# Attention and a gated mixer in one kernel: row sums from a ones column in V, scalings on two engines, V's rows ordered by SBUF loads

## The chip, the cores and the metric

The kernel runs on one core of a Trainium2 chip. A core has five engines that run their own instruction lists side by side: TensorE (PE; its weight loads are listed as PEld), VectorE (DVE), ScalarE (ACT), GpSimd (POOL) and SyncE (SP, which here only issues transfers). SBUF is the core's memory of 128 partitions; PSUM, eight banks of 2 KB per partition, takes the results of TensorE. The metric is the device time of one execution in microseconds (us), lower is better.

## The reference

There are 2048 tokens of width 448 in bf16. First comes an attention block: every token looks at eight tokens, itself and those 2, 4, ..., 14 positions before it. Then comes a gated mixer whose spatial product mixes all 2048 tokens.

```
def _A_ref(x, wqkv, wo):                 # H = 16 heads of Dh = 28
    W, dil = (8, 2)
    qkv = (x @ wqkv).reshape(B, S, 3, H, Dh) ...
    idx = pos[:, None] - (arange(W) * dil)[None, :];  mask = idx >= 0
    logits = einsum('bhsd,bhswd->bhsw', q, k[idx]) * Dh ** -0.5
    attn = softmax(where(mask, logits, -1e9))
    return einsum('bhsw,bhswd->bhsd', attn, v[idx]) ... @ wo

def _B_ref(x, w_in, w_sp, b_sp, w_out):  # Fh = 896
    z = gelu(x @ w_in);  z1 = z[..., :Fh];  z2 = layernorm(z[..., Fh:])
    g = einsum('ts,bsf->btf', w_sp, z2) + b_sp[None, :, None]
    return (z1 * g) @ w_out

h  = x + _A_ref(layernorm(x), wqkv, wo)
h2 = h + _B_ref(layernorm(h), w_in, w_sp, b_sp, w_out)
```

## The kernel before, in words

**Layout.** The 2048 tokens are 16 blocks of 128. A unit u (0 to 7) is the pair of blocks u and u + 8. xh (L421) holds the normalized input transposed: features on partitions, the first 1024 tokens on partitions 0 to 63 and the second 1024 on 64 to 127, so that two products with a contraction of 64 stand side by side for the two halves. The work goes from the last unit to the first.

**First layer norm (ln_unit, L634).** For each block statistics on VectorE (bn, L640, L645), 1/sqrt(var + eps) on POOL (L629, L630) or on ScalarE as Ln and Exp (L656, L657), and the scaling to tring on VectorE (nrm, L664). Then the transpose: units 7, 6 and 5 on PE with a copy from PSUM, units 4 to 0 by a DMA transpose issued on SP (L671). The second layer norm, of h, uses the same function with all eight units transposed by DMA. Blocks wait in a ring of four tring buffers.

**Q, K and V.** Q and K are computed in three chunks of tokens (L776) from padded weights wpd, which VectorE and ScalarE copy out of staged loads. V is computed in nine tiles of 114 tokens with a halo of 14 (L826). Since the attention looks at every second token, a tile's V must stand with even tokens on partitions 0 to 63 and odd ones on 64 to 127. To get this, the kernel before copies the tile's columns of xh, reordered, into xv (L816; two buffers, on VectorE or ScalarE), and uses xv as the stationary operand. V itself is copied from PSUM into one of three buffers (L838) whose heads are 32 wide: 28 values and four zeros.

**A tile of attention (i = 8 down to 0).** Two groups of 32 logit products (mml, L857), two Exp (L871) into E, two multiplies by the band mask on VectorE (L879), eight products of E with a matrix of ones (mmr, L892), which give each row's sum on all 32 rows of its head, a Ln and an Exp(-x) on ScalarE for the reciprocal in L (L901, L926), 64 value products E times V (mmo, L915), and the multiply by the reciprocal out of PSUM into oT on VectorE (ot, L934).

**Behind it.** For each unit the output projection (mmy, L978), the residual add into x_tm (h, L987), the second layer norm, two z2 groups (L999) with a GELU on ScalarE (L1009), the statistics of z2 (L1015, L1021) and its scaling (nrm3, L1029, VectorE). The z1 groups (L1042) have their own GELU (L1052). Then the spatial product g (L1076) in 28 groups of 16, the bias add and the gate on VectorE (L1086, L1093), and the output product (L1103), add (L1111) and store (L1115). The transposed loads of w_sp (L959) are chained: each waits for the one before it.

**What sets the order.** Every piece of work is a task. SEQ (L48) gives, for each of the five engines, the order of its tasks, written out by number. replay (L299) walks these lists with estimated costs, hands out PSUM banks and ring buffers, and records the instructions; each engine runs its list in order and waits on semaphores where it must. All loads, transposes and stores but two stand in SP's one list. When PE waits for long at the start, replay puts in matmuls on a constant tile to keep PE's clock (L618).

## Time and profile before

| | |
|---|---|
| median of three runs | 242.56 us (242.48 to 242.93) |
| the profiled execution | 242.51 us |
| its span | 240.8 us |
| granted clock of TensorE | 1.00 |
| PE busy | 233.3 us, 97% |
| VectorE busy | 136.7 us, 57% |
| ScalarE busy | 91.1 us, 38% |
| POOL busy | 24.9 us, 10% |
| moved by DMA | 22.52 MB |

The page gives busy time by engine, groups of equal instructions ("L879 DVE TENSOR_TENSOR out<-in" with its count, the busy time, the mean in ns of one, the idle time before and what ended it), and the chain that ended last. In a table of windows each row is a stretch of the span in us with the busy time and count of instructions of every engine in it, PE's granted clock, the busy share of the DMA engines and GB/s. A line of the timeline gives start, duration, engine, line, operation, tile and count. Lines of transfers give KB each and the us from issue to landing. Matmuls overlap, so that the sum of the durations of single ones is more than the time of a group; the chain has the time of a group.

### The profile page before, as it was taken

Reading aid. Unit: us, or ns where it says so; the run is one execution under the profiler, and the core shown is the slowest. Engines: PE = TensorE matmul, PEld = TensorE weight load, DVE = VectorE, ACT = ScalarE, POOL = GpSimd, SP = SyncE. Lnnn points to the kernel's source line nnn. Section 1 sums busy time; section 2 is a strip of 40 time slices with the busy share of each in tenths; the row PEclk is TensorE's granted clock in tenths of the full one; section 3 lists DMA queues with packets and bytes.
Section 4 is the critical chain, followed back from the end, with each engine's and each line's share of the span. In section 5 each row is a group of like instructions: output and inputs, shape, how many; then the busy total and the mean of one; then the engine's idle time right before and its main releaser. Section 6 shows DMA issues by size and latency. Waiting matters only on the chain.

```text
span 240.8 us, 6345 instructions
## 1 busy us (share of the span) xinstructions
PE 233.3 (97%) x2838; PEld 122.0 (51%) x2838; DVE 136.7 (57%) x288; ACT 91.1 (38%) x108; POOL 24.9 (10%) x66
## 2 busy tenths in 40 slices
PE   8889999999999999999999999999999999999994
PEld 2567754545556655555444444444444444444552
DVE  4989667699999995194951012235115522053743
ACT  2899877669998458965430000000000000000000
POOL 7114100001111133025120000000000000000000
PEclk9999999999999999999999999999999999999999
DMA  6959995293294959776844333000000100000034
GB/s 179 298 180 151 189 185 110 67 220 71 46 124 86 203 164 156 159 134 131 158 94 94 74 80 73 0 0 3 0 0 0 57 3 0 0 0 3 0 114 135
DMA packets 56558, 22.52 MB, mean 94 GB/s; under 512 B 46930, under 2 KB 56402, under 8 KB 56530
## 3 DMA queue, kind: packets, MB, share of 16 engines
q1 hardware_dynamic: 56242, 21.88, 43.6%
q8 instruction: 22, 0.36, 0.6%
q10 hardware_dynamic: 288, 0.23, 0.3%
q14 instruction: 6, 0.05, 0.1%
HBM read 8.90 MB, written 1.84 MB: 45 GB/s over the span
## 4 chain that ended last, share of the span: by engine, by line
PE 83%; DVE 9%; DMA 3%; SPq 2%; issue 1%; ACT 0%; DVEq 0%
PE psum L1076 40%; PE psum L776 9%; PE psum L999 9%; PE psum L1042 9%; PE psum L1103 6%; PE psum L826 4%; PE psum L978 3%; DMA z2p<-in_A_wqkv_dram 2%; DVE x_tm L987 2%; DVE st L640 2%; DVE reg L934 1%; DMA out_dram<-tring 1%; DVE reg L879 1%; PE psum L857 1%; PE psum L915 1%
## 5 line engine op out<-in xcount | busy, mean ns | idle before, releaser
L1086 DVE TENSOR_TENSOR reg<-psum,reg 128x512 bf16<-128x512 f32 x28 | 18.7, 687 | 62.2 <-PE psum L1076 62.1
L1076 PE MATMUL psum<-wspT_lo,z2p 128*128 128x512 bf16 x224 | 49.3, 379 | 0.0
L1076 PE MATMUL psum<-reg,z2p 128*128 128x512 bf16 x224 | 49.3, 379 | 0.0
L1076 PEld LDWEIGHTS psum<-wspT_lo,z2p 128*128 128x128 bf16 x224 | 21.8, 98 | 26.5 <-DVE st L1015 0.4
L1076 PEld LDWEIGHTS psum<-reg,z2p 128*128 128x128 bf16 x224 | 21.9, 98 | 26.3
L776 PE MATMUL psum<-xh,reg 64*128 64x256 bf16 (+2 forms) x336 | 25.6, 306 | 1.2 <-DVE reg L626 0.6
L999 PE MATMUL psum<-w_in,xh 64*128 64x448 bf16 x224 | 22.5, 349 | 0.1
L1103 PE MATMUL psum<-reg 128*128 128x448 bf16 (+1 forms) x119 | 22.3, 341 | 0.0
L1042 PE MATMUL psum<-xh,w_in 64*128 64x512 bf16 x196 | 21.9, 376 | 0.0
L1015 DVE BATCH_NORM_STATS2 st<-z2p 128x6 f32<-128x448 bf16 x32 | 17.7, 609 | 7.1 <-ACT z2p L1009 7.1
L776 PEld LDWEIGHTS psum<-xh,reg 64*128 64x128 bf16 x336 | 16.2, 94 | 9.2 <-DVE reg L626 1.2
L640 DVE BATCH_NORM_STATS2 st<-x_tm 128x6 f32<-128x448 bf16 x32 | 18.9, 613 | 2.3 <-DMA x_tm<-in_A_x_dram 2.2
L624 ACT ACTIVATE reg<-psum 128x1024 bf16<-128x1024 f32 (+2 forms) x19 | 17.1, 917 | 4.8 <-PE psum L776 4.7
L1052 ACT ACTIVATE reg<-psum 128x1024 bf16<-128x1024 f32 x14 | 13.8, 1029 | 12.2 <-PE psum L1042 12.2
L1111 DVE TENSOR_TENSOR tring<-psum,x_tm 128x448 bf16<-128x448 f32 (+1 forms) x17 | 9.6, 592 | 15.1 <-PE psum L1103 13.3
L871 ACT ACTIVATE reg<-psum 128x928 bf16<-128x928 f32 x18 | 16.2, 943 | 4.0 <-PE psum L857 4.0
L999 PEld LDWEIGHTS psum<-w_in,xh 64*128 64x128 bf16 x224 | 12.4, 94 | 9.0 <-issue 0.6
L1103 PEld LDWEIGHTS psum<-reg 128*128 128x128 bf16 x119 | 11.6, 98 | 10.0
L1042 PEld LDWEIGHTS psum<-xh,w_in 64*128 64x128 bf16 x196 | 11.1, 94 | 9.9 <-ACT reg L1052 0.2
L630 POOL TENSOR_TENSOR rs<-rs,nhalf 128x2 f32<-128x2 f32 x20 | 14.9, 746 | 1.7
L1009 ACT ACTIVATE z2p<-psum 128x896 bf16<-128x896 f32 x16 | 13.8, 927 | 3.2 <-PE psum L999 3.1
L629 POOL TENSOR_SCALAR rs<-mv 128x2 f32<-128x2 f32 x20 | 5.1, 254 | 94.1 <-DVE mv L645 71.7
(59 smaller groups left out, 201.6 us busy)
## 6 DMA issues: line engine op xcount, KB each, us to landing
w_in<-in_B_w_in_dram SPq DMA_DIRECT2D x4, 672.0 KB, 5.8
out_dram<-tring SPq DMA_DIRECT2D x15, 112.0 KB, 1.8
x_tm<-in_A_x_dram SPq DMA_DIRECT2D x6, 224.0 KB, 5.6
z2p<-in_A_wqkv_dram SPq DMA_DIRECT2D x3, 336.0 KB, 5.6
reg<-in_B_w_out_dram SPq DMA_DIRECT2D x1, 784.0 KB, 4.5
reg<-in_A_wqkv_dram SPq DMA_DIRECT2D x2, 336.0 KB, 6.1
reg<-in_B_b_sp_dram SPq DMA_DIRECT2D x1, 512.0 KB, 5.5
w_in<-in_B_w_in_dram SPq DMA_DIRECT2D x4, 112.0 KB, 4.8
```

The costliest lines, as they stand in the source:

```text
L624: iss("act", lambda e: e.activation(dst, src, AF.Copy), reads=rd, writes=wr)
L630: iss("pool", lambda e: e.tensor_tensor(dst, dst, nh, ALU.pow), reads=rr + [r_nhalf], writes=rr)
L640: iss("dve", lambda e: e.bn_stats(st[:, b, :], x_tm[:, b, :]), reads=[r_x[b]], writes=[rl[b]])
L776: iss("pe", lambda e, k=k, s=s, gi=gi, lhs=lhs: e.matmul(psum[:, bk[s] * 512 + cw * gi:bk[s] * 512 + cw * gi + cw], lhs, xh[64 * s:64 * s ...
L871: iss("act", lambda e: e.activation(E[:, es[0], 2 * n:2 * n + 2, :], pair_view(lb, 8 * JW), AF.Exp, scale=SCALE), reads=[r_bank[lb[0]], r_ ...
L999: iss("pe", lambda e, c=c, s=s: e.matmul(psum[:, zb[s] * 512:zb[s] * 512 + D], xh[64 * s:64 * s + 64, ROWS[s][c], HX + 128 * u:HX + 128 * ...
L1009: iss("act", lambda e: e.activation(z2p[:, u:u + 9:8, D * k:D * k + D], pair_view(zb, D), AF.Gelu_apprx_tanh), reads=[r_bank[zb[0]], r_ban ...
L1015: iss("dve", lambda e, b=b: e.bn_stats(st3[:, b, k, :], z2p[:, b, D * k:D * k + D]), reads=[r_z2[b][k]], writes=[r_st3[b][k]])
L1042: iss("pe", lambda e, c=c, s=s: e.matmul(psum[:, bk[s] * 512:bk[s] * 512 + 512], w_in[64 * s:64 * s + 64, c, 128 * f:128 * f + 128], xh[64 ...
L1076: iss("pe", lambda e, b=b: e.matmul(psum[:, gb[0] * 512:gb[0] * 512 + 512], z2p[:, b, 128 * f:128 * f + 128], src[:, b, 512 * (tc % 2):512 ...
L1086: iss("dve", lambda e: e.tensor_tensor(ub[:, us_[0], :], psum[:, gb[0] * 512:gb[0] * 512 + 512], bb[:, 512 * tc:512 * tc + 512], ALU.add), ...
L1103: iss("pe", lambda e, f=f: e.matmul(psum[:, wb[0] * 512:wb[0] * 512 + c1 - c0], z1p[f][:, 128 * m:128 * m + 128], w_out[:, f, c0:c1], star ...
```

## The change

- **Row sums.** Each head of V gets a column of ones at place 28 (c_V now writes zeros to 28..31 and then 1.0 to 28). The value product then yields the row sum in row 28 of every head's 32 rows. mmr, the ones matrices and their PSUM pair are gone. A stream_shuffle on VectorE (sh) copies row 28 over all 32 rows, from PSUM into L; Ln and Exp run in L. For tile 0 a POOL memset clears the ones of the halo tokens.
- **V's rows.** V is computed straight from xh, in the order of tokens, copied from PSUM into a buffer Vt (two of them), and two SBUF to SBUF loads on SP move the even and the odd rows of Vt into V. xv and its copies are gone. 18 loads are added.
- **Scalings.** The second layer norm's scaling and that of z2 may run on ScalarE (scale: Identity with scale and bias); POOL then works out the bias, -mean times rstd (shift). By the new order six of 16 of each kind run there.
- **The start.** The statistics of block 14 come from two ScalarE activations with accumulation; unit 6's seven transposes are split four and three over two banks with a copy each; K's weights are loaded once, as Q's were, and put in place by three copies per half, not one; two larger loads bring wo, after a VectorE memset of its padding; the copy of wo2 to the upper partitions stands on ScalarE.
- **The order.** SEQ is a new one throughout. Per tile PE now has the 64 value products in one piece. Around the last three tiles ScalarE switches between the tables of Exp and GELU: it has six table loads in all, before four.

```diff
-XV_ON = ("dve", "act")
+NVT = 2
+ONCE = "qk"
+ACT_STAT = (14,)
+SPLIT_T = (6,)
 SEQ = (
...
-        c_V = cst("c_V", [(lambda e, v=v: e.memset(V[:, v, :, :, DH:32], 0.0), [], [r_V[v]]) for v in range(NV)], 0.75, deps=[c_ident])
+        c_V = cst("c_V", [(lambda e, v=v, a=a, b=b, x=x: e.memset(Vt[:, v, :, :, a:b], x), [r_vt[v]] if x else [], [r_vt[v]])
+                          for v in range(NVT) for a, b, x in ((DH, 32, 0.0), (DH, DH + 1, 1.0))], 0.9, deps=[c_ident])
...
+        def shift(name, u, nb, mv, rs, rl, tr, users):
+
+            def em():
+                bs = [b for b, t in users if t.eng == "act"]
+                for b in bs:
+                    iss("pool", lambda e, b=b: e.tensor_tensor(nb[:, b:b + 1], mv[:, b, 0:1], rs[:, b:b + 1], ALU.mult), reads=[rl[b]], writes=[r_nb[name][b]])
+                for b in bs:
+                    iss("pool", lambda e, b=b: e.tensor_scalar(nb[:, b:b + 1], nb[:, b:b + 1], -1.0, None, ALU.mult),
+                        reads=[r_nb[name][b]], writes=[r_nb[name][b]])
+            return add("%s_%d" % (name, u), "pool", 0.8, em, deps=[tr])
+
+        def scale(t, dst, src, nb, mv, rs, b, rd, rn, wr):
+            if t.eng == "act":
+                iss("act", lambda e: e.activation(dst, src, AF.Identity, scale=rs[:, b:b + 1], bias=nb[:, b:b + 1]), reads=rd + [rn], writes=wr)
+            else:
+                iss("dve", lambda e: e.tensor_scalar(dst, src, mv[:, b, 0:1], rs[:, b:b + 1], ALU.subtract, ALU.mult), reads=rd, writes=wr)
...
-            def em(a=a, xs=xs, rx=rx, tk=tk):
+            def em(a=a, bk=bk, rx=rx):
                 o = HX - HALO + a
-                copy(tk[0].eng, xv[:, xs[0], :, :].rearrange("p c (w j) -> p c w j", w=2),
-                     xh[:, :, o:o + 128].rearrange("p c (j w) -> p c w j", w=2), rx, [r_xv[xs[0]]])
...
-                            xv[64 * s:64 * s + 64, xs[0], ROWS[s][k], :],
+                            xh[64 * s:64 * s + 64, ROWS[s][k], o:o + 128],
                             wv[64 * s:64 * s + 64, k, :], start=(k == 0), stop=(k == NC7 - 1)),
...
-                copy(tk[0].eng, V[:, vs[0], :, :, 0:DH], pair_view(bk, D).rearrange("p s (h d) -> p s h d", d=DH),
+                copy(tk[0].eng, Vt[:, vt[0], :, :, 0:DH], pair_view(bk, D).rearrange("p s (h d) -> p s h d", d=DH),
...
+            if i == 0:
+                def em(vt=vt):
+                    iss("pool", lambda e: e.memset(Vt[0:HALO, vt[0], 0, :, DH:DH + 1], 0.0), writes=[r_vt[vt[0]]])
+                tv = add("v0", "pool", 0.1, em, deps=[tv])
+            for w in range(2):
+                tv = dma("sp", "vd%d_%d" % (i, w), lambda e, w=w, vs=vs, vt=vt: e.dma_start(V[64 * w:64 * w + 64, vs[0]], Vt[w:128:2, vt[0]]),
...
-            def em(i=i, es=es, rb=rb):
-                for s in range(2):
-                    on = ones0 if i == 0 and s == 0 else ones
...
-            tr = add("mmr%d" % i, "pe", 0.25, em, deps=tks + [c_ones], acq=[("ps", 2, rb)], mode="O", nmm=8)
...
-                iss("act", lambda e: e.activation(L[:, ls[0], :, :], pair_view(rb, 8 * JW), AF.Ln),
...
+            def em(ob=ob, ls=ls):
+                iss("dve", lambda e: e.stream_shuffle(L[:, ls[0], :, :], pair_view(ob, 8 * JW), [DH] * 32),
+                    reads=[r_bank[ob[0]], r_bank[ob[1]]], writes=[r_L[ls[0]]])
+            tr = add("sh%d" % i, "dve", 1.12, em, deps=[to], acq=[("L", 1, ls)])
+
+            def em(ls=ls):
+                iss("act", lambda e: e.activation(L[:, ls[0], :, :], L[:, ls[0], :, :], AF.Ln),
```

More of the change, by code (lines that the diff above doesn't have):

```diff
@@ L510, in bass_sequential_preLN__sliding_local_dilated__mixer_gmlp__prompt_kernel @@
         r_ln3 = [Res("ln3_%d" % b) for b in range(NB)]
+        r_nb = {n: [Res("%s_%d" % (n, b)) for b in range(NB)] for n in ("nb2", "nb3")}
         reg1_old = [r for p in "qk" for rr in r_w[p] for r in rr] + r_ld["v"]
@@ L641, in ln_unit @@
                 tb.append(add("bn%d_%d" % (which, b), "dve", 0.53, em, deps=[src_deps[n]] + ([c_warm] if which == 1 else [])))
+            bd = [b for b in bl if which == 2 or b not in ACT_STAT]
             def em():
-                for b in bl:
+                for b in bd:
                     iss("dve", lambda e, b=b: e.bn_aggr(mv[:, b, :], st[:, b, :]), reads=[rl[b]], writes=[rl[b]])
-            ta = add("ag%d_%d" % (which, u), "dve", 0.20, em, deps=tb)
+            ta = add("ag%d_%d" % (which, u), "dve", 0.10 * len(bd), em, deps=[t for n, t in enumerate(tb) if bl[n] in bd])
             tk = []
@@ L765, in bass_sequential_preLN__sliding_local_dilated__mixer_gmlp__prompt_kernel @@
                 p = "q" if isq else "k"
-                rows = ROWS_Q if isq else ROWS
+                rows = ROWS_1 if p in ONCE else ROWS
                 for g0 in range(0, 4, per):
                     bk = []
-                    rx = [r_xh[b] for b in us] + ([r_xpad] if (t0 == 0 and not isq) else [])
+                    rx = [r for b in us for r in r_xh[b]] + ([r_xpad] if (t0 == 0 and not isq) else [])
                     def em(t0=t0, cw=cw, g0=g0, bk=bk, per=per, off=off, p=p, rx=rx, rows=rows):
@@ L1124, in bass_sequential_preLN__sliding_local_dilated__mixer_gmlp__prompt_kernel @@
         for n, t in enumerate(ld_in):
-            t.deps.append(t_xh[4 - n // 2])
-        chain([t_wsp[b][0] for b in S_ORDER], t_xh[0])
+            t.deps += t_xh[4 - n // 2]
+        chain([t_wsp[b][0] for b in S_ORDER], t_xh[0][0])
         chain([t_wsp[b][1] for b in S_ORDER], t_wout)
```

200 lines of the change are left out of this document (109 added, 91 removed), and 61 rows, old and new, of the table SEQ.

## The prediction

> **What bounds the kernel now.** I read the page's busy shares first, then the table of windows, then the chain that ended last, then groups by shape. The profiled execution took 242.51 us, its span 240.8, so 1.7 us lie around the span; the median of the three runs is 242.56, and the sum below is made against 242.51. A change of 0.2% (0.5 us) is about what a measurement of this kernel can tell from none.
>
> ```profile
> PE 233.3 (97%) x2838; PEld 122.0 (51%) x2838; DVE 136.7 (57%) x288; ACT 91.1 (38%) x108; POOL 24.9 (10%) x66
> ```
> ```profile
> core 0: us, PE busy (x) PEld busy (x) DVE busy (x) ACT busy (x) POOL busy (x), PEclk, DMA share, GB/s
> 9.24:21.11 11.87, 11.17 (x275) 8.21 (x275) 10.70 (x34) 10.70 (x17) 1.04 (x3) 1.00 0.86 188
> 21.11:50.00 28.89, 28.14 (x748) 17.34 (x740) 21.11 (x28) 22.83 (x27) 3.15 (x6) 1.00 0.73 146
> 50.00:93.00 43.00, 42.31 (x972) 23.91 (x968) 41.58 (x86) 33.23 (x38) 8.40 (x18) 1.00 0.71 128
> 93.00:119.62 26.62, 26.62 (x264) 14.53 (x259) 16.38 (x44) 17.03 (x19) 5.91 (x12) 1.00 0.78 154
> 119.62:232.00 112.38, 112.38 (x539) 52.42 (x538) 37.49 (x77) 2.85 (x3) 1.52 (x2) 1.00 0.13 31
> ```
>
> TensorE is the bound nearly everywhere, at a granted clock of 1.00. Whatever leaves its queue in the first 120 us is a gain, unless a wait takes its place. VectorE is full beside it from 50 to 93 (41.58 of 43.00) and has 7.8 us free from 21 to 50; ScalarE has 9.8 free from 50 to 93. From 119.62 on there is only the spatial product, which the change leaves as it is but for the order of its last groups.
>
> **The change part by part.** Prices of what is removed, and of the PE groups used as cover, from the chain that ended last (start, us, what):
>
> ```profile
> 31.48 0.64 PE psum L915 x64
> 37.90 0.73 PE psum L857 x59
> 41.76 0.32 PE psum L892 x8
> 70.99 1.62 PE psum L978 x16
> 83.92 1.32 PE psum L999 x14
> 85.24 1.51 PE psum L1042 x14
> 106.47 4.53 PE psum L1042 x42
> ```
>
> *Row sums (-2.9).* Nine groups of eight matmuls against the ones leave PE: 9 x 0.32 = 2.9 us. The sums now come out of the value product itself, row 28 of every head, at no PE time. PE is 98% busy where they stood, so I count all of it.
>
> *The shuffle (on VectorE).* The reciprocal's chain was beside the value product; now it begins behind it: shuffle, Ln, Exp, multiply.
>
> ```profile
> L934 DVE TENSOR_TENSOR reg<-psum,reg 128x912 bf16<-128x912 f32 x9 | 11.0, 1222 | 2.5 <-ACT reg L926 2.5
> L879 DVE TENSOR_TENSOR reg<-reg,mband 128x928 bf16<-128x928 bf16 x18 | 11.1, 631 | 1.6 <-ACT reg L871 1.6
> L926 ACT ACTIVATE reg<-reg 128x928 f32<-128x928 f32 x9 | 8.8, 976 | 0.2
> L626 DVE COPY xv<-xh 128x896 bf16<-128x896 bf16 x3 | 3.2, 1069 | 0.3 <-PE psum L826 0.3
> L624 ACT ACTIVATE xv<-xh 128x896 bf16<-128x896 bf16 x5 | 4.8, 958 | 0.0
> L626 DVE COPY reg<-reg 64x3584 bf16<-64x3584 bf16 x1 | 1.1, 1087 | 0.0
> L664 DVE TENSOR_SCALAR tring<-x_tm,mv,rs 128x448 bf16<-128x448 bf16 x32 | 11.6, 385 | 2.1 <-POOL rs L630 1.5 <-ACT rs L657 0.3
> L629 POOL TENSOR_SCALAR rs<-mv 128x2 f32<-128x2 f32 x20 | 5.1, 254 | 94.1 <-DVE mv L645 71.7 <-DVE mv L1021 21.8 <-POOL rs L630 0.3
> ```
>
> No row has a shuffle. From below the bf16 multiply of its size bounds it (0.63), from above twice the float32 PSUM read of L934 (2.4); I take 1.2, L934 itself, the only row with its source, width and type. Nine make 11 us more on VectorE. Off it go three xv copies (3.2), the copy of wo2 (1.1) and six of the sixteen second scalings (6 x 0.385 = 2.3): net some 4.5 us; one V copy more (1.1) stands against a first statistic and some Q/K copies less. I lay it into the 7.8 us free between 21 and 50, for in the new order four tiles' shuffles and multiplies stand between the Q/K copies there; behind tile 5's multiply VectorE's list is then the old one plus 5 x 1.2 - 2 x 1.07 - 2.3 = +1.6.
>
> By the Trainium skill, page "VectorE: DVE Perf Modes", section "The perf-mode tier table (the rule you actually need)", a shuffle runs at the single rate, about 2400 ns for 2048 elements; my estimate from it for 928 is 1.1 us, and the sum would stay as it is. No run here shows it yet.
>
> *PSUM (+1.0).* A tile's product keeps its pair of banks through shuffle, Ln, Exp and multiply: 1.2 + 0.98 + 0.98 + 1.2 = 4.4 us, where the sums kept theirs for one Ln and the product only waited for the multiply. The floor is 0 (another pair is free). The other end is 2.0: the last two tiles, where the GELU input also sits in banks while ScalarE swaps tables, wait an Exp each. I take 1.0.
>
> *V's rows (0, while 8.3 us cover it).* The xv copies go (ScalarE -4.8); V is evacuated to Vt, and two SBUF loads of 128 KB place even and odd rows.
>
> ```profile
> x_tm<-in_A_x_dram SPq DMA_DIRECT2D x2, 112.0 KB, 2.5
> w_in<-in_B_w_in_dram SPq DMA_DIRECT2D x4, 112.0 KB, 4.8
> wspT_lo<-in_B_w_sp_dram SPq DMA_TRANSPOSE x16, 3.6
> xh<-tring SPq DMA_TRANSPOSE x13, 4.1
> ```
> ```profile
> 21.53 0.48 SPq L947 DMA_DIRECT2D reg<-in_A_wo_dram  x1
> ```
> ```profile
> L671 SPq DMA_TRANSPOSE xh<-tring x13: 1223/1296/2078, 16.6 to 94.7; - x13
> ```
>
> These are 18 more issues on SP's queue (0.5 each), in one order with the w_sp transposes, each of which waits until the one before has landed (3.6), and with the xh transposes, which wait for VectorE or ScalarE. A load behind such a wait is late with it, and the value product after it, and all that PE has queued behind that product. Path per tile: copy to Vt 1.0, first issue 0.5, one transpose between the two loads, landing of the second. No row has a load from SBUF to SBUF; of 112 KB rows the fastest landed in 2.5, those among the bulk loads in 4.8. Low: 1.0 + 0.5 + 1.3 (issue of a transpose) + 2.5 = 5.3. High: 1.0 + 0.5 + 3.6 (a chained transpose waited out) + 4.8 = 9.9. Cover: what stands in PE's new order between a tile's V product and its value product. At tile 3 that is two and a half logit blocks of 64 (1.8), two output projections (3.2), two V products (2.6, shape and count of the L999 groups) and one value product (0.6): 8.3; tile 8 has about the same, tile 6 8.6, tile 2 9.3, the others more. I take the path at 7.6, the middle: hidden by 0.7.
>
> *The start (-1.0, then +0.7).* K's weights come with one 336 KB load fewer, unit 6's transposes are evacuated in two halves by two engines, and one block's statistics move to ScalarE.
>
> ```profile
> 9.24 3.27 PE L776 MATMUL psum<-xh,reg 64*128 64x256 bf16 x56 [0.55 <-DVE xh L626]
> 13.12 3.23 PE L776 MATMUL psum<-xh,reg 64*128 64x256 bf16 x56 [0.61 <-DVE reg L626]
> ```
> ```profile
> 12.44 1.15 DVE L626 COPY reg<-z2p 128x1568 bf16<-128x1568 bf16 x2 [0.46 <-DMA z2p<-in_A_wqkv_dram]
> ```
> ```profile
> L626 DVE COPY reg<-z2p 64x672 bf16<-64x672 bf16 x3 | 1.2, 386 | 0.1
> L626 DVE COPY xh<-psum 128x896 bf16<-128x896 bf16 x1 | 0.6, 618 | 0.0
> ```
> ```profile
> 10.94 1.04 DVE st L640 x2
> 52.64 1.01 DVE x_tm L987
> ```
> ```profile
> 16.55 3.23 SPq L671 DMA_TRANSPOSE xh<-tring  x2
> ```
>
> The wait of 0.61 on K's copies (which waited on the weights, 0.46) goes, and one statistic (0.52) less ahead of unit 6 lets the first group start 0.4 earlier: -1.0. But PE then comes to the second Q/K chunk at 20.1 instead of 21.11, and that needs unit 4, whose DMA transpose was issued at 16.55 and takes 4.1. VectorE has a little more ahead of unit 4's scaling: one statistic 0.5, two small copies 0.8, a half evacuation 4/7 x 0.62 = 0.35, less the two copies of 1.15 and 0.4 of idle time, some 0.2 with an aggregate. Issue 16.75, landing 20.85, a wait of about 0.7 (0 if VectorE keeps its pace by having fewer gaps, 1.5 if the transposes land late as 4.8 after issue).
>
> *The rest.* Six second scalings and six of z2 on ScalarE, each behind two small POOL products (2 x 0.25, beside the queue). The cover: before, unit 0 landed at 94.7 + 4.1 = 98.8 and was first needed at 106.5; now PE has, from the last output projection on, four z1 groups, four z2 groups and unit 1's two: 6.0 + 7.9 = 13.9 us. VectorE's list from there to unit 0's scaling is a residual add 1.0, eight statistics 4.2 and three scalings 1.2, 6.5 with an aggregate; the issue of another transpose in front 1.3, the landing 4.1: 11.9. Slack 2.0, no term. At the end the last store is a half block:
>
> ```profile
> L1111 DVE TENSOR_TENSOR tring<-psum,x_tm 128x448 bf16<-128x448 f32 x15 | 9.1, 620 | 15.1 <-PE psum L1103 13.3 <-DMA out_dram<-tring 1.8
> L1111 DVE TENSOR_TENSOR tring<-psum,x_tm 128x224 bf16<-128x224 f32 x2 | 0.8, 380 | 0.0
> ```
>
> 0.380 - 0.620 = -0.2. ScalarE also has two table loads more, interleaved between the last tiles:
>
> ```profile
> 76.30 1.28 ACT L524 ACT_TABLE_LOAD   x1
> 77.59 2.53 ACT L1009 ACTIVATE z2p<-psum 128x896 bf16<-128x896 f32 x3
> ```
>
> By these rows a switch costs 1.28, and the GELU starts 0.01 after it. Two make 2.6. ScalarE further takes the copy of wo2 (four times 128x896 wide: 3.8 by the xv copy's 0.958 per 896) and six scalings (about 0.5 each, 3.0), and loses six xv copies (5.7): some +4 over the whole stretch from 21 to 93, where it has 6.1 + 9.8 free. No term, but its Ln and Exp are now in the path of rival 4.
>
> **Sum.** -2.9 + 1.0 + 0 - 1.0 + 0.7 - 0.2 = -2.4: 242.5 - 2.4 = 240.1.
>
> **Rivals.**
> 1. *More goes than I count.* No PSUM wait (-1.0), unit 4 in time (-0.7), and the waits that PE still has from 21 to 93 (0.75 + 0.69 = 1.4 by the windows) half filled by the new order: 240.1 - 2.4 = 237.7. For it: VectorE's free time before 50. Against: it is full afterwards. Chance 0.18, down to 236.5.
> 2. *V's rows come late* (slower): at the high end, 9.9, tiles 8 and 3 wait 1.6 each, tile 6 1.3, tile 2 0.6: 5.1, so 245.2. It decides from a path of some 9.2 on, where 0.9 + 0.9 + 0.6 eats the 2.4. For it: DMA is 0.71 to 0.86 busy there, one queue. Against: 2.5 on an empty queue. Chance 0.15.
> 3. *VectorE becomes the bound.* At 2.4 a shuffle, tile 5 onward is 5 x 1.2 = 6 later, the 2.0 of slack go: +4.0, 244.1. Below some 1.6 a shuffle it does not show. Chance 0.12.
> 4. *The table switches.* Two tiles' Ln and Exp now stand between GELUs. If a switch took twice the load, 2 x 1.28, four of them would bring unit 0 5.1 later: with 2.0 of slack +3.1, 243.2. The rows above show nothing behind a load. Chance 0.03. The Trainium skill, page "ScalarE: Activation LUTs", section "What ACT_TABLE_LOAD costs", gives this rule: about 1.28 us of load plus 1.38 of drain for every switch; the trace agrees with the first figure and shows nothing of the second.
> 5. *The gain is waited away*: PE waits 2.4 longer somewhere for what the ones matmuls bridged: 242.5. Chance 0.10.
>
> **Numbers.** My forecast, 238.7 to 241.8, has 0.42. Faster: 0.42 + 0.18 + 0.02 of case 5 = 0.62; same 0.06; slower 0.15 + 0.12 + 0.03 + 0.02 = 0.32. The range, 236.8 to 245.2, leaves out the ends of cases 1 and 2, some 0.1 each.
>
> **What would show it.** Right: no ones matmuls; the shuffle at 1.1 to 1.3; PE's second chunk near 21; the spatial product starting near 117.4 instead of 119.69; PE idle under 2 us from 21 to 93. Wrong: a PE wait before the value products released by a DMA (rival 2), VectorE still at second scalings past 94 (3), ScalarE gaps at table loads (4), PE waiting for multiplies that free banks beyond 1 us.

## The result, and the profile after

The changed kernel takes 245.14 us (median, 244.95 to 245.52), the kernel before, beside it on the same chip, 242.52: a ratio of 1.0118, 95% interval 1.0085 to 1.0151. It is slower by 1.2%; I had forecast 240.1, and the other sign. The profiled execution took 245.52, its span 243.8, that is 3.0 more than the span before. Here and below a median is that of all runs of a kernel, and a ratio leaves out the runs that took over 1.5% more than the fastest of the same kernel.

Lines of the changed kernel: L837 Q/K, L876 V product, L898 V's loads from Vt, L919 logits, L933 their Exp, L958 value product, L968 shuffle, L973 and L978 Ln and Exp, L986 multiply, L1027 output projection, L1036 residual add, L1048 z2, L1130 spatial product; L631 and L633 are copies on ScalarE and VectorE.

The table of windows after, at the bounds of before and then from the first Q/K group to the spatial product; columns as before:

```profile
core 0: us, PE busy (x) PEld busy (x) DVE busy (x) ACT busy (x) POOL busy (x), PEclk, DMA share, GB/s
9.24:21.11 11.87, 11.81 (x293) 10.22 (x295) 11.65 (x35) 10.52 (x15) 3.82 (x8) 1.00 1.00 209
21.11:50.00 28.89, 25.61 (x628) 15.21 (x626) 22.86 (x35) 20.26 (x22) 1.23 (x2) 1.00 1.00 185
50.00:93.00 43.00, 40.77 (x962) 21.62 (x960) 37.56 (x70) 38.92 (x44) 8.46 (x23) 0.96 0.62 108
9.27:123.12 113.85, 108.31 (x2170) 61.09 (x2170) 97.50 (x205) 90.93 (x101) 26.67 (x67) 0.99 0.79 150
```

The same stretch of the kernel before:

```profile
9.24:119.62 110.38, 108.24 (x2241) 63.99 (x2242) 89.77 (x188) 83.79 (x98) 18.50 (x38) 1.00 0.75 145
```

The spatial product starts at 123.12 instead of 119.62, 3.5 later; from there to the end the changed kernel is 0.5 shorter. PE, with 71 fewer matmuls in the record, is busy as long as before (108.31, 108.24), and its idle time went from 2.14 to 5.54. DMA is busy 1.00 instead of 0.73 from 21 to 50, and the clock is below full from 50 to 93. PE's waits, grouped, after (us in total, times, longest):

```profile
PE psum L876 <- issue: 2.2, 1, 2.2
PE psum L837 <- DVE reg L633: 0.8, 1, 0.8
PE psum L958 <- DVE x_tm L1036: 0.8, 1, 0.8
PE psum L1048 <- ACT reg L933: 0.7, 1, 0.7
PE psum L837 <- issue: 0.6, 2, 0.3
PE psum L1027 <- ACT Vt L631: 0.4, 1, 0.4
PE psum L919 <- DVE Vt L633: 0.3, 1, 0.3
PE psum L919 <- issue: 0.3, 1, 0.3
PE psum L958 <- DMA reg<-Vt: 0.2, 1, 0.2
```

and before:

```profile
PE psum L776 <- DVE reg L626: 0.6, 1, 0.6
PE psum L776 <- DVE xh L626: 0.5, 1, 0.5
PE psum L826 <- DVE reg L934: 0.5, 1, 0.5
PE psum L915 <- DVE reg L934: 0.3, 1, 0.3
PE psum L857 <- issue: 0.2, 1, 0.2
PE psum L857 <- DVE x_tm L987: 0.2, 1, 0.2
```

"Issue" is a wait for nothing that the program asks for: 0.2 before, 3.0 after. Waits for PSUM banks (those for a multiply, a residual add, an Exp of logits or a copy of V) are 0.9 before and 2.1 after (0.76, 0.65, 0.38, 0.28). The waits of 0.8 after (for L633) and 0.5 before (for xh) end where the first Q/K group begins; the stretch starts there, and its idle time does not hold them. The places that count most, in the timeline of PE after:

```profile
36.06 0.35 PE L876 MATMUL psum<-reg,xh 64*128 64x448 bf16 x1
38.57 1.49 PE L876 MATMUL psum<-reg,xh 64*128 64x448 bf16 x13 [2.16 <-issue]
69.05 0.67 PE L958 MATMUL psum<-reg 64*32 64x58 bf16 x64 [0.76 <-DVE x_tm L1036]
70.75 2.16 PE L1048 MATMUL psum<-w_in,xh 64*128 64x448 bf16 x14 [0.65 <-ACT reg L933]
```

The first wait stops PE in the middle of a V product, between two matmuls that wait for the same things. What SP had issued just before, and how long the loads took:

```profile
30.57 0.60 SPq L563 DMA_DIRECT2D w_in<-in_B_w_in_dram  x1
32.81 0.59 SPq L563 DMA_DIRECT2D w_in<-in_B_w_in_dram  x1
35.66 2.51 SPq L563 DMA_DIRECT2D w_in<-in_B_w_in_dram  x2
```
```profile
w_in<-in_B_w_in_dram SPq DMA_DIRECT2D x4, 672.0 KB, 8.3
reg<-Vt SPq DMA_DIRECT2D x18, 128.0 KB, 4.7
```

By the Trainium skill, page "Runtime: NRT & Kernel Launch", section "Instruction fetch mechanics", an engine draws its program in blocks of 16 KB through a DMA queue of its own, a cost "mostly hidden". The profile has such packets, 21 of 16 KB:

```profile
q8 instruction: 21, 0.34, 0.7%
```

The trace keeps the start and the end of each one. The packet at this stall runs from 35.80 to 37.19; PE goes on at 38.57, 1.38 behind its end. In the profiled runs of all 17 kernels PE's timeline from 9 to 125 us has 41 issue waits, of 0.16 us or more. Of these, 38 end 1.2 to 2.0 us behind the end of such a packet; the other three, of 0.16 each, stand at the start of the spatial product. So these waits are PE's program coming late, and that the cost is hidden does not hold here. From 24 to 80 us the 22 packets with a wait of 0.5 us or more behind them took no longer than the 155 with none (1.13 and 1.12 us on average): they began too late. In the 2 us before such a packet the DMA engines had been busier, 0.97 against 0.71 on average. That busy DMA is what delays their start is argued from this and from experiment 1; no row shows when a packet was asked for.

The second place, the waits of 0.76 and 0.65, follows from ScalarE, which after 66.8 stood 1.18 before it could copy V of tile 0, for both Vt buffers still waited for their loads:

```profile
67.99 0.92 ACT L631 ACTIVATE Vt<-psum 128x896 bf16<-128x896 f32 x1 [1.18 <-PE psum L1027]
```

(PE's projection, which the row names, had long ended.) Behind it the clock falls to a half for some 3.4 us, and the z2 product at 70.75 takes 2.16 instead of 1.50:

```profile
71.00:72.00 1.00, 1.00 (x12) 0.54 (x10) 1.00 (x1) 1.00 (x3) 0.00 (x0) 0.72 0.05 8
72.00:73.00 1.00, 1.00 (x18) 0.27 (x18) 1.00 (x4) 0.95 (x2) 0.00 (x0) 0.50 0.46 92
73.00:74.00 1.00, 1.00 (x36) 0.62 (x34) 0.78 (x2) 0.48 (x1) 0.00 (x0) 0.50 0.88 138
74.00:75.00 1.00, 1.00 (x8) 0.40 (x6) 0.00 (x0) 1.00 (x2) 0.00 (x0) 0.57 0.37 131
```

Low clock cannot be what makes the median: two of the four runs had a mean clock of 1.000 and took 245.26 and 244.95. What they lost in its place no profile shows.

### The profile page after: what moved, and what is told of

The parts are those of the page before. It is cut to its first block, busy times and chain, and to the rows that moved or that the text cites. A ratio compares the mean times of both kernels' runs of the same rounds, so it can differ in the third digit from the quotient of the medians.

```text
span 243.8 us, 6266 instructions
## 1 busy us (share of the span) xinstructions
PE 233.6 (96%) x2765; PEld 119.1 (49%) x2765; DVE 141.6 (58%) x295; ACT 103.0 (42%) x117; POOL 32.0 (13%) x92
## 3 DMA queue, kind: packets, MB, share of 16 engines
HBM read 8.50 MB, written 1.84 MB: 42 GB/s over the span
## 4 chain that ended last, share of the span: by engine, by line
PE 82%; ACT 6%; DVE 3%; DMA 2%; issue 2%; POOL 2%; SPq 1%; ACTq 0%; POOLq 0%; DVEq 0%
PE psum L1130 40%; PE psum L837 10%; PE psum L1157 9%; PE psum L1096 8%; PE psum L1048 7%; PE psum L876 3%; DMA reg<-Vt 2%; PE psum L1027 2%; ACT L529 2%; ACT z2p L1058 1%; PE psum L919 1%; ACT reg L978 1%; ACT Vt L631 1%; PE psum L958 1%; DVE reg L986 1%
## 5 line engine op out<-in xcount | busy, mean ns | idle before, releaser
L1130 PE MATMUL psum<-reg,z2p 128*128 128x512 bf16 x224 | 49.0, 379 | 0.0
L1130 PE MATMUL psum<-wspT_lo,z2p 128*128 128x512 bf16 x224 | 48.7, 379 | 0.0
L1130 PEld LDWEIGHTS psum<-wspT_lo,z2p 128*128 128x128 bf16 x224 | 21.8, 98 | 26.6 <-DVE z2p L655 0.4
L1130 PEld LDWEIGHTS psum<-reg,z2p 128*128 128x128 bf16 x224 | 21.9, 98 | 26.3
L837 PE MATMUL psum<-xh,reg 64*128 64x256 bf16 (+2 forms) x336 | 26.0, 306 | 1.4 <-DVE reg L633 0.8
L1048 PE MATMUL psum<-w_in,xh 64*128 64x448 bf16 x224 | 24.0, 364 | 0.7 <-ACT reg L933 0.7
L837 PEld LDWEIGHTS psum<-xh,reg 64*128 64x128 bf16 x336 | 16.9, 94 | 9.0 <-ACT xh L631 1.2
L682 DVE BATCH_NORM_STATS2 st<-x_tm 128x6 f32<-128x448 bf16 x31 | 18.2, 613 | 0.5 <-DMA x_tm<-in_A_x_dram 0.5
L933 ACT ACTIVATE reg<-psum 128x928 bf16<-128x928 f32 x18 | 16.4, 941 | 2.4 <-PE psum L919 2.3
L1048 PEld LDWEIGHTS psum<-w_in,xh 64*128 64x128 bf16 x224 | 11.2, 97 | 11.5 <-issue 2.0
L636 POOL TENSOR_SCALAR rs<-mv 128x2 f32<-128x2 f32 x22 | 5.9, 269 | 82.0 <-DVE mv L689 71.7
L637 POOL TENSOR_TENSOR rs<-rs,nhalf 128x2 f32<-128x2 f32 x22 | 16.0, 726 | 1.8
L876 PE MATMUL psum<-reg,xh 64*128 64x448 bf16 x126 | 13.6, 350 | 2.2 <-issue 2.2
L1096 PEld LDWEIGHTS psum<-xh,w_in 64*128 64x128 bf16 x196 | 9.4, 94 | 11.5 <-ACT z2p L1058 0.4
```

The source lines that it names most:

```text
L637: iss("pool", lambda e: e.tensor_tensor(dst, dst, nh, ALU.pow), reads=rr + [r_nhalf], writes=rr)
L682: iss("dve", lambda e: e.bn_stats(st[:, b, :], x_tm[:, b, :]), reads=[r_x[b]], writes=[rl[b]])
L837: iss("pe", lambda e, k=k, s=s, gi=gi, lhs=lhs: e.matmul(psum[:, bk[s] * 512 + cw * gi:bk[s] * 512 + cw * gi + cw], lhs, xh[64 * s:64 * s ...
L876: iss("pe", lambda e, k=k, s=s: e.matmul(psum[:, bk[s] * 512:bk[s] * 512 + D], xh[64 * s:64 * s + 64, ROWS[s][k], o:o + 128], wv[64 * s:64 ...
L933: iss("act", lambda e: e.activation(E[:, es[0], 2 * n:2 * n + 2, :], pair_view(lb, 8 * JW), AF.Exp, scale=SCALE), reads=[r_bank[lb[0]], r_ ...
L1048: iss("pe", lambda e, c=c, s=s: e.matmul(psum[:, zb[s] * 512:zb[s] * 512 + D], xh[64 * s:64 * s + 64, ROWS[s][c], HX + 128 * u:HX + 128 * ...
```

## The experiments

In the diffs the lists of SEQ are written by the tasks' names: win1_1 is a load of w_in, wsp one of w_sp, vd one of V's rows, tD a transpose. All ratios are to the kernel before.

**1. Are w_in's loads too close together?**

e1_spread:

```diff
 SP
-wsp0_7, win0_1, win0_0, vd4_0
+wsp0_7, vd4_0
-wsp0_14, vd3_1
+wsp0_14, win0_0, vd3_1
-tD2_6, win0_3
+tD2_6, win0_1, win0_3
```

> The changed kernel with two of the four 672 KB loads of w_in moved back on SP's queue: the third behind the w_sp transpose of block 14 (48.7 us there), the fourth in front of w_in's last two small loads (73 us). Theory A (PE's own instructions are fetched late behind the four bulk loads that stand together from 30.6 to 36.3 us): PE's wait of 2.16 us at 36.4 for nothing in the program falls under 0.5, the median to about 243.2. Rival B (the loads that place V's rows delay the fetch, or PE waits there for something else): that wait stays above 1.5, the median at 245 +- 0.5.

e4_before_bunched, from the kernel before:

```diff
 SP
-win1_1, wo0, tD1_1, tD1_0, tD1_2, wsp0_7, win1_0
+wo0, tD1_1, tD1_0, tD1_2, wsp0_7, win1_1, win1_0, win0_1, win0_0
-win1_3, win0_0, win1_2
+win1_3, win1_2
-tD2_4, win0_1, win0_3
+tD2_4, win0_3
```

> The kernel before, unchanged but for SP's order: its four 672 KB loads of w_in (19.8, 31.6, 48.8, 77.3 us there) stand one behind the other at about 31 us, as in the changed kernel; nothing waits for them earlier than it did. Theory A: PE waits 1.5 to 2.5 for nothing in the program within some 8 us behind them, where it waited 0.2 in all, the median 244 to 245. Rival B (bulk loads do not matter to PE's fetch; V's loads do): that wait stays under 0.4, the median at 242.5 +- 0.4.

e4 measured 245.10, 1.0113 (1.0076 to 1.0150): four loads moved in SP's order, and the kernel before is as slow as the changed one. Its PE waited, where it had waited 0.2:

```profile
PE psum L857 <- issue: 1.8, 3, 1.2
PE psum L857 <- DVE reg L626: 0.8, 1, 0.8
```

This is theory A in kind, and roughly in size: 1.25 of the 1.8 came within 8 us of the loads, and the median is 0.1 above its range. The 0.8 is another cost of the same move: in SP's ordered queue wo's last load was issued at 44.84 instead of 40.80, and VectorE stood 1.24 for it. Idle time is 1.6 longer than before; PE is also busy 1.0 longer for the same work, for which no row gives a reason. But e1 took 245.50, 1.0126 (1.0084 to 1.0168). In its profiled run, the slowest of its four (247.44), the wait at 36 us fell to 0.90, and others came: 1.59 in a V product at 61.6, behind the moved load and w_in's small ones, 1.38 for V's first load, and 1.84 for the last w_in load, which I had moved too far back. The bunching is enough to stall PE; with V's loads there, taking it away is not enough.

**2. Are two Vt buffers too few?**

e2_vt3, and e3_spread_vt3 with e1's order as well:

```diff
-NVT = 2
+NVT = 3
-        Vt = sb("Vt", [128, NVT, 2, 16, 32], BF16)
+        Vt = z2flat[:, 8 * FH:8 * FH + NVT * 1024].rearrange("p (v s h d) -> p v s h d", v=NVT, s=2, h=16)
-                        reads=[r_bank[zb[0]], r_bank[zb[1]]], writes=[r_z2[u][k], r_z2[u + 8][k]], after=stage_old)
+                        reads=[r_bank[zb[0]], r_bank[zb[1]]], writes=[r_z2[u][k], r_z2[u + 8][k]], after=stage_old + (r_vt if u < 4 else []))
```

> The changed kernel with three buffers Vt instead of two (placed in z2p's blocks 8 to 11, which are written after 80 us). Theory C (ScalarE is held at 68 us by a copy into a Vt buffer whose load has not landed, PE then waits 0.76 and 0.65 for what is queued behind it, and the granted clock falls to 0.5 to 0.7 from 71 to 75 us because of those gaps): ScalarE's wait of 1.18 goes, PE's two waits fall under 0.3 together, the clock stays above 0.95 in that stretch; -1.1 for the waits and -1.7 for the clock, the median about 242.3. Rival D (the loads' landing itself, some 6 us, is what is late, and a third buffer only moves the wait to the value product): PE waits 0.5 to 1.5 at the value products of tiles 1 or 0 instead, the median 244.5 to 245.5.

> Both edits together. If A and C hold and are independent: 245.1 - 2.0 - 2.8 = about 240.3, below the kernel before. If only A holds: 243. If only C: 242.3. If neither: 245.

e2: 243.93, 1.0068 (1.0035 to 1.0101), some 1.2 better than the changed kernel, though the two intervals overlap. ScalarE's wait of 1.18 is gone, PE's two waits are 0.17 and 0.37, and the clock is full from 50 to 93. So C holds for these waits and for the clock there. PE's waits for banks are now 0.9 in all, as in the kernel before. The time gains less than 2.8, for PE's issue waits are now 3.5, and the clock was 0.94 from 21 to 50, behind one of 2.72:

```profile
38.83 2.17 PE L876 MATMUL psum<-reg,xh 64*128 64x448 bf16 x13 [2.72 <-issue]
```

e3: 245.07, 1.0119 (1.0066 to 1.0172): issue waits of 4.7, the longest 2.14 in a logit block at 66.6. The two gains do not add.

**3. The row sums without V's loads.**

e5_copies and e6_copies_spread (the latter with w_in's loads apart):

```diff
-            tv = add("evv%d" % i, "act", 0, em, deps=[tm, c_V], acq=[("vt", 1, vt)], rel=[("ps", bk)],
+            tv = add("evv%d" % i, "act", 0, em, deps=[tm, c_V], acq=[("V", 1, vs)], rel=[("ps", bk)],
...
-            for w in range(2):
-                tv = dma("sp", "vd%d_%d" % (i, w), lambda e, w=w, vs=vs, vt=vt: e.dma_start(V[64 * w:64 * w + 64, vs[0]], Vt[w:128:2, vt[0]]),
+            tk.append(add("xv%d" % i, "act", 0.88, em, acq=[("xv", 1, xs)], deps=[t for b in us for t in t_xh[b]] +
```

> The changed kernel with V's rows put in place as before (a copy xv of each tile's columns, with the even ones first, ahead of its V product; V is evacuated straight into V), so without Vt and the 18 loads of 128 KB; row sums by the ones column, shuffle and all the rest stay. The order of the ScalarE, VectorE and TensorE lists was shifted by a few places each so that the copies fit. SP's order is that of the changed kernel less the 18 loads, the four 672 KB loads still together. Theory E (V's loads, by being late and by holding ScalarE, cost the waits at the value products and from 69 to 75 us): PE's waits for reg<-Vt and at 69 to 71 and the low clock go, -2.8, the bunched loads still cost some 2: 242.3. Rival F (the row sums' new chain through VectorE is what costs): 244 to 245.5, with PE waiting on VectorE's multiplies instead.

> The same with the four 672 KB loads apart, at about 31, 35, 50 and 65 us. Theory A and E together: PE's waits for nothing in the program under 0.7 in all, the median near my forecast without the V path, 240.3. Rival F: 242.5 or more. If A is wrong: as e5_copies.

e5: 244.95, 1.0116 (1.0073 to 1.0159); e6: 244.44, 1.0087 (1.0061 to 1.0113). By their times both go with F, but of what F names, PE waiting for multiplies, the record of e5 has 0.4 and that of e6 nothing. The profiled run of e6, its fastest at 243.12, has no issue wait over 0.2, and its stretch to the spatial product is

```profile
9.29:120.47 111.18, 106.66 (x2170) 59.35 (x2170) 96.62 (x206) 94.18 (x108) 27.04 (x66) 1.00 0.64 133
```

PE busy 1.6 less than before, idle 4.5 instead of 2.1: 1.7 for transposes of xh, 1.2 at a Q/K chunk, 1.0 for banks, the rest under 0.2 each. The 1.2 is put down to an Exp that frees a bank, but w_sp's first load, which waits for unit 0's transpose, could be issued just then (35.38), and the chunk needs that transpose too. So all but the banks is, as I read it, of my order, which had the transposes late; e6's median is 1.3 above this run, and no profile shows where the other runs lost it.

**4. V's loads, apart and as dummies.**

e7_vt3_four (e2 with w_in's loads at four places) and e8_before_dummy:

```diff
 SP (e7)
-win1_0, vd5_1, wsp0_7, win0_1, win0_0, vd4_0, wsp0_15, vd4_1, wsp0_6, vd3_0, wsp0_14
+vd5_1, wsp0_7, win1_0, vd4_0, wsp0_15, vd4_1, win0_1, wsp0_6, vd3_0, wsp0_14, win0_0
```
```diff
+        for n in range(18):
+            dma("sp", "dd%d" % n, lambda e, n=n: e.dma_start(Vd[64 * (n % 2):64 * (n % 2) + 64, 1 + n // 2 % 2], Vd[n % 2:128:2, 0]), 64 * 2048,
+                deps=[c_vd], reads=[r_ds], writes=[r_dd[n % 4]], bw=150.0, setup=0.5)
```

> The changed kernel with three Vt buffers and the four 672 KB loads apart, at about 30, 36, 44 and 50 us, ahead of stretches of Q/K products; the small ones stay. Theory A (only the bunching delays the fetch): PE's waits for nothing in the program under 1.0 in all, the median 241.5 to 242. Rival G (all transfers together do, V's loads among them, where 64 matmuls take 0.7 us; apart or not, a fetch meets one of them): these waits stay at 2 to 4 in all at other places, the median 243.5 to 245.

> The kernel before, with 18 loads more of the shape of V's (64 partitions of 2 KB, SBUF to SBUF, from a zeroed buffer into spare space), at the times in SP's order at which the changed kernel issues V's; nothing waits for them, the result does not use them. Theory G: traffic alone delays PE's fetch and other landings; PE's waits for nothing in the program 1 to 2.5 in all instead of 0.2, the median 243.3 to 244.7. Theory E in its narrow form (V's loads cost only where a consumer waits for them): 242.2 to 242.8, issue waits under 0.5.

e7: 245.74, 1.0133 (1.0068 to 1.0199), with issue waits of 3.3, the longest 1.62 at 37.7 and 1.65 at 60.6, each inside a V product: G, not A alone, and the median is above the range of G too. e8: 250.56, 1.0350 (1.0304 to 1.0395), far above all I had expected. Its issue waits are only 1.1. What it lost is SP's order: the dummies and what they wait for pushed wo's last load back by 6 us (46.9 instead of 40.8), VectorE stood for it in front of its copy of wo2, and PE behind VectorE:

```profile
50.32 1.09 DVE L629 COPY reg<-reg 64x3584 bf16<-64x3584 bf16 x1 [4.37 <-DMA reg<-in_A_wo_dram]
```
```profile
52.71 0.92 PE L860 MATMUL psum<-reg 28*64 28x58 bf16 x64 [3.83 <-DVE reg L629]
```

Behind that wait the clock was at a half from 50.9 to 57.7, which takes up to 3.4 more. So e8 does not price traffic by itself; it shows what 18 issues in one ordered queue do to those behind them.

**5. What the ones matmuls cost.**

```diff
-                for s in range(2):
+                for s in (0, 1, 0, 1):
                     on = ones0 if i == 0 and s == 0 else ones
```

> The kernel before, with the eight ones matmuls of each tile issued twice (the second time over the same banks with the same result), nothing else changed. It prices what the change takes off TensorE. My prediction's step: a group costs its 0.32 of the chain, so +2.9 and a median of 245.2. Theory H, from the starts in the timeline (a group of ones begins 0.21 to 0.25 ahead of the group behind it; the rest of its 0.37 runs under that group): +1.9 to 2.3, a median of 244.2 to 244.6. From the difference of PE's busy time between the kernel before and e6_copies_spread (1.6): 243.9.

245.41, 1.0114 (1.0072 to 1.0156): 2.8 with an interval of 1.7 to 3.8. It holds the first two guesses and not the third, 1.6. The profiled run, at 244.10 the fastest of six, has PE busy 109.53 in the stretch instead of 108.24:

```profile
9.08:121.24 112.16, 109.53 (x2314) 62.95 (x2314) 90.03 (x188) 84.10 (x98) 18.44 (x38) 1.00 0.75 143
```

1.3 of work, and 0.5 more idle time (issue waits of 1.3). With e6's 1.6 that puts the work, as PE's busy time has it, at 1.3 to 1.6. By the times of the runs it is not settled: five of the six took 0.3 to 2.3 longer than the profiled one, and no profile shows why. The timeline of the kernel before says why the work can be less than 2.9:

```profile
41.69 0.39 PE L892 MATMUL psum<-reg,ones 64*32 64x464 bf16 x8
41.90 0.45 PE L915 MATMUL psum<-reg 64*32 64x58 bf16 x32
```

The group behind starts 0.21 after the ones; the rest of their 0.39 lies under it.

**6. Orders laid anew.** In e10, e11 and e12 the lists from 8 to 112 us were laid again, with durations as the traces show them:

```diff
+        for x in pl.tasks:
+            n = x.name
+            x.setup += 1.3 if n[:2] == "tD" else 3.0 if n[:2] == "vd" else 0.3 if n[:3] == "wsp" else 0
+            if n[:3] == "nrm" and x.alts and "act" in x.alts:
+                x.alts["act"] += 0.25
...
         pl.replay()
```

> e6_copies_spread (row sums by the ones column and the shuffle, V's rows by copies, w_in's loads apart) with its waits of 1.17 at 35.4 us (unit 0's transposes came late), 1.5 for xh and 0.5 for an Exp worked on: the order of the lists is laid anew with the durations that the traces show (scalings on ScalarE 0.76 and 1.12, transposes landing 1.3 later, the memset of wo2 1.55), and POOL takes unit 7's reciprocal root ahead of the band mask. If nothing is left but the row sums (-1.6 to -2), the start and the end (-0.5): 240 to 241, faster than the kernel before. If the shuffle's chain holds PSUM so that PE waits wherever the order is put: 242 to 243.5, with 3 to 5 us of PE's waits between 9 us and the spatial product.

> The changed kernel with three Vt buffers and w_in's loads apart, its lists laid anew in the same way as in e10, with V's loads landing 3 us later than the order had allowed for (they landed 4.7 after issue in the median). Theory G (V's loads cost by their traffic, whatever the order): PE's waits for nothing in the program stay at 2 to 4 us, the median 243 to 245, 2 to 4 above e10. Theory K (the order alone was wrong, made for loads of 1.4 us): waits for V's loads and ScalarE's blocks go and the median comes within 1 us of e10.

> e10_copies_relaid with its lists laid once more, against ScalarE and VectorE durations 7% longer and later landings, so that small delays do not reach PE: its waits of 1.14 for banks from 67 to 70 us are to go, and with them the low clock from 69.5 to 73. If order is all that is left: PE's waits under 2.5 in all, a median of 241 to 241.8, faster than the kernel before. If the shuffle's chain, by holding a product's banks some 6.5 us instead of some 4.3, keeps PE waiting in any order: 242 to 243.5, as e10.

e10 (V by copies): 242.69, 1.0008 (0.9972 to 1.0044), no slower and no faster than before, with PE idle 3.66 in the stretch, as its second guess had it:

```profile
9.81:121.44 111.63, 107.97 (x2169) 62.84 (x2169) 99.17 (x210) 92.64 (x105) 26.85 (x62) 0.98 0.68 125
```

e11 (V by loads): median 246.29, ratio 1.0111 (1.0067 to 1.0154). The ratio counts six of its 12 runs, with a median of 244.8; by these it is 2.1 above e10, by the two ratios 2.5. K does not hold; the time is that of G, though not by issue waits (1.9, where e10 has 1.4 and e12, without V's loads, 2.3). A lowered clock is part of it: 10 of e11's 12 runs had one against 6 of e10's. Among runs at full clock the two are 1.2 apart (243.1 from two runs, 241.9 from six). The orders of e10 and e11 were laid apart, so they differ in more than V's path. e12: 245.96, 1.0137 (1.0081 to 1.0193), above both its guesses. The waits that e12 was to remove were 0.59 and 1.35 at 68 to 71 us, and an issue wait of 1.97 came at 38.

e15_copies_hand, three moves in e10:

```diff
 ScalarE
-nrm2_15, evv0, exp1_0, ln3, exp1_1, rex3
+nrm2_15, ln3, evv0, exp1_0, exp1_1, rex3
 VectorE
-nrm2_13, sh2, ot3
+nrm2_13, ot3, sh2
```

> e10_copies_relaid with three moves: on ScalarE tile 3's Ln goes ahead of V's last evacuation (into 0.5 of idle time) and the second Exp of tile 1 ahead of tile 3's Exp, on VectorE tile 3's multiply goes ahead of tile 2's shuffle, so that the pair of banks that tile 3's product holds from 60 to 71 us comes free about 1 us earlier. If banks are what PE waits for there: 1.14 falls to 0.4 to 0.7, the clock stays up in more runs than e10's 6 of 12, a median of 241.5 to 242.3. If not: as e10, 242.7, or worse where the moves make another wait.

243.19, 1.0047 (1.0021 to 1.0072), no better than e10. The waits for banks there fell from 1.14 to 0.70 and the clock was full in all 12 runs; a wait of 1.22 for a multiply at 75 us took their place, and issue waits of 2.0 instead of 1.4. In none of the orders tried was PE idle under 3.6 in this stretch.

**7. Does a wait lower the clock?** e13_before_gate and e14_before_wait, from the kernel before:

```diff
-                            reads=rot + r_wo, writes=[r_bank[bk[s]]])
+                            reads=rot + r_wo + ([r_x[3]] if u == 2 else []), writes=[r_bank[bk[s]]])
-            tm = add("mmy%d" % u, "pe", 16 * mm_rate(D), em, deps=t_ot[i0:tl_ + 1] + t_wo, acq=[("ps", 2, bk)], mode="P", nmm=16)
+            tm = add("mmy%d" % u, "pe", 16 * mm_rate(D), em, deps=t_ot[i0:tl_ + 1] + t_wo + ([pl.named["h3"]] if u == 2 else []), acq=[("ps", 2, bk)], mode="P", nmm=16)
```

(e13 has the first change alone.)

> The kernel before, with unit 2's output projection (70.9 us) made to wait for unit 3's residual add as well (ends 72.8), a wait of 1.8 to 2 on TensorE right behind the last blocks of small matmuls. Theory L (a wait of that length there lets the granted clock fall for some 3 us, as after 71 us in the changed kernel): a clock of 0.5 to 0.7 for 2 to 4 us behind it in some of the runs, those with a mean clock of 0.993 some 1.5 longer than the others; medians of 244 to 246. Rival (the low clock has another cause): the clock stays 0.998 or more in all runs, the median 243.9 to 244.4.

> The kernel before, with unit 2's output projection (70.9 us) made to wait for the end of unit 3's residual add (72.8): one wait of 1.8 to 2 on TensorE, right behind the last blocks of small matmuls. Theory L (such a wait lets the granted clock fall for some 3 us): a mean clock of 0.993 or less in half of the runs or more, as in the kernels whose PE was busy 1.0 to 2.2 of the 3 us from 67 to 70 (2 of 4, 6 of 12, 10 of 12, 6 of 6), those runs 1.5 to 2 longer than the others; a median of 244.5 to 246. Rival (the low clock has another cause): 0.998 or more in nearly all runs, the median 243.7 to 244.4.

In e13 the edit did not do what I meant: the projection was recorded first, so the add waited for it. 243.10, 1.0049 (1.0013 to 1.0084), one run of 12 at a clock of 0.993. e14 has the wait, with one filler matmul in it:

```profile
71.79 0.39 PE L618 MATMUL psum<-warm 128*128 128x512 bf16 x1 [0.85 <-ACT reg L871]
72.70 1.69 PE L978 MATMUL psum<-reg 64*128 64x448 bf16 x16 [0.52 <-DVE x_tm L987]
```
```profile
70.00:73.00 3.00, 1.62 (x49) 0.76 (x47) 3.00 (x6) 2.70 (x4) 0.28 (x1) 1.00 0.83 129
```

244.00, 1.0080 (1.0056 to 1.0104), as the rival had it; the clock was full in all six runs. Idle time of 1.4 in 3 us, in these two pieces, did not lower it. The last section shows a reason why this test does not settle the matter.

## Why the prediction was wrong, step by step

The step that failed is the price of nothing for the new transfers: V's rows at 0, and no term for w_in's loads in their new places. In their place the profile after shows PE's program coming late (issue waits +2.8) and PE and ScalarE held up by Vt buffers whose loads had not landed (waits of 0.76 and 0.65 on PE).

The account of the two spans: work on PE about -1.5, low clock +1.6 (the z2 groups take 24.0 instead of 22.5 in all), issue waits +2.8, banks +1.2, the wait of 0.61 inside the first Q/K groups gone, V's loads +0.2, other small waits -0.2, from the spatial product on -0.5; together +3.0. It is an account of the one profiled run; two of the four runs had no low clock and took as long.

- **Row sums, -2.9: too large by PE's busy time.** That has 1.3 to 1.6 (experiments 3 and 5); the time of experiment 5, 2.8 (1.7 to 3.8), leaves the size open. I took the step of the chain, a group's time to its end, for what PE would have free; its start to the start behind it was 0.21.
- **The shuffle, 1.2: right.** VectorE is busy 4.9 longer in all (I had said 4.5).

```profile
L968 DVE STREAM_SHUFFLE reg<-psum 128x928 f32<-128x928 f32 x9 | 10.7, 1192 | 0.0
```

- **PSUM, +1.0: the size right by luck.** PE waited 1.2 more for banks, but 1.41 of its 2.1 are the two waits behind the Vt buffers. With a third buffer (e2) the waits for banks are 0.9, as before. I had a pair held for the four operations, 4.4. From the start of a tile's value product to the end of its multiply I find 6.9 on average after and 4.3 before; tile 3 after from 61.30 to 72.09:

```profile
61.30 0.78 PE L958 MATMUL psum<-reg 64*32 64x58 bf16 x64
```
```profile
70.89 1.20 DVE L986 TENSOR_TENSOR reg<-psum,reg 128x912 bf16<-128x912 f32 x1
```

  The four stand in the lists of two busy engines, and wait there between one another. In e2 the hold is as long (6.8) and costs PE nothing more than before; in e10, at 8.3, the waits for banks are 1.9.
- **V's rows, 0: failed.** As a latency it was nearly right: one value product waited 0.2 for a load. I priced 18 loads by when they land and by SP's issue time, and not by what they are besides: traffic (issue waits), and holders of the two Vt buffers (ScalarE's 1.18, PE's 0.76 and 0.65). e11 over e10 puts V by loads at 2.1 to 2.5 us, of them 1.2 where the clock was full; e2 puts the missing third buffer at some 1.2, with intervals that overlap.
- **w_in's loads, no term: failed.** I read their new places in the order and gave them no price. e4 shows that this alone costs the kernel before 1.1%, as much as the whole change. Taking such costs away one at a time does not add up (e3).
- **The start, -1.0 then +0.7: better than said.** The second Q/K chunk began at 20.16 instead of 21.11, and unit 4 was in time. The first group did not begin earlier (9.27): unit 7's root waited on POOL for the band mask until 5.06, which I had not followed. The gain is behind it: the wait of 0.61 is gone, and PE is busy 11.81 of the 11.87 us from 9.24 on, where it was 11.17.
- **ScalarE, no term: right in effect.** Its scalings took 0.76 and 1.13, not my 0.5, but no wait of PE is put down to them.

```profile
L653 ACT ACTIVATE z2p<-z2p,nb,rs 128x896 bf16<-128x896 bf16 x6 | 6.5, 1126 | 0.0
L653 ACT ACTIVATE tring<-x_tm,nb,rs 128x448 bf16<-128x448 bf16 x6 | 4.6, 759 | 0.0
```

- **The last store, -0.2:** the stretch behind the spatial product's start is 0.5 shorter.

Of the rivals, 2 has the time (245.2) but not the mechanism: value products hardly waited. 3 did not come at 1.19 a shuffle, 4 not at table loads of 1.28 with the next operation 0.01 behind:

```profile
79.42 1.28 ACT L529 ACT_TABLE_LOAD   x1
80.71 0.98 ACT L973 ACTIVATE reg<-reg 128x928 f32<-128x928 f32 x1
```

5, the gain waited away, is nearest, with more waited away than gained. Of the signs of being right, "PE idle under 2 us from 21 to 93" failed: it was 5.5. And 0.2% was too little for the noise: the 79 runs of the kernel before that stand beside the experiments took 241.3 to 246.4, and the intervals above are 0.2% to 0.7% to each side.

What stays open: the runs of e5, e6 and e9 that took 1 us or more over their profiled one; what the runs after at full clock lost; why the clock falls; and how much of e10's idle time belongs to the longer hold of banks and how much to its order. A version faster than both kernels was not found.

## What to carry to other kernels

Loads that nothing waits for are not free (e4): before a change moves or adds DMA, look at what PE draws from its program then, and at every load queued behind. Before you price work taken off the bound engine by its duration, look how far apart the starts are (0.21 for groups of 0.39 here). When a result in PSUM gets one more step on a busy engine, count the queue in front of each step, not the steps' sum (6.9 against 4.4); whether that costs anything depends on what else holds the banks.

## What the hardware showed that I had not expected

PE stalls in the middle of a product for up to 2.7 us (e2), because its program comes late. In the four longest of these waits (2.72 in e2, 2.16 after, 2.14 in e3, 1.97 in e12) the packet of 16 KB had begun only 0.04 to 0.74 us before PE stopped. Summed over the stretch, such waits were 1.9 to 4.7 in the six kernels with V's loads and 0 to 2.3 in those without, dummies aside; the kernel before with its four big loads together had 1.9, apart 0.2. So V's loads are not needed for such a stall.

The clock is 0.50 for 3.41 us near 70 us in the profiled runs of the changed kernel, e10 and e12; a run with one such stretch has a mean clock of 0.993. By that mean it fell in 2 of 4 runs after, 6 of 12 of e10, 10 of 12 of e11, 6 of 6 of e12, and 3 of 79 of the kernel before; the median of e10's runs is 243.8 with it and 241.9 without, e11's 246.5 and 243.1. In the changed kernel and in e10 it came behind a stretch in which PE was idle here and there (e10: 1.86 busy of the 3 us from 67). The changed kernel:

```profile
64.00:71.00 7.00, 5.32 (x196) 3.29 (x196) 6.35 (x15) 5.45 (x7) 2.76 (x7) 1.00 0.93 151
```

The trace keeps the times at which the clock changed. In the six profiled runs with a half clock before the spatial product (after, e1, e2, e8, e10, e12) it begins a whole number of steps of 3.413 us (19, 17, 10, 13, 19, 19) behind the moment at which the clock first rose to full. In the step just before, PE was busy 0.69 to 2.27 us. But after the first step twelve others up to 125 us had as little (1.58 to 2.25) and the clock stayed full, among them one of e11 from 64.85; so PE's busy share alone does not decide. In e14's profiled run a border of two steps falls at 72.19, between its two pieces of idle time: no step had both. A test with all of it in one step is missing.

The Trainium skill, page "TensorE: Matmul & The Clock Gate", section "What's actually happening", has only a full and a half clock, and a window of about 3.4 us; the 0.50 and the 3.41 us of this case agree with it. Its table has the half clock come behind at least one idle window; if that means a gap of that length, it does not fit: in the changed kernel and e10 no single gap in front of it was over 0.8 us.
